# The ninth half rows of the second up projection on 64 partitions, three quarters of them loaded by GpSimd

## The chip, the cores and the metric

One NeuronCore of a Trainium2 chip runs the whole program. The metric is the device time of one execution in microseconds (us). PE is the matrix engine, DVE the vector engine, ACT the scalar engine, POOL is GpSimd, SP the engine that issues most transfers. In the profile PEld is PE's loading of weights.

## The reference

Two layers of a decoder, run twice with the same weights, for one token in each of two sequences. All data are float32.

```python
B, Sq, D = 2, 1, 576            # x
H, Sk, Dh = 32, 8192, 128       # caches: 2 x 32 x 8192 x 128, twice (K and V)
Df = 4608
def _A_ref(x, k_cache, v_cache, wq, wo):      # attention on a cache
    q = (x @ wq) as B, H, 1, Dh
    p = softmax(q . k_cache * Dh ** -0.5)
    return (p . v_cache) as B, 1, H * Dh @ wo
def _B_ref(x, w_gate, w_up, w_down):          # gated MLP
    return (gelu(x @ w_gate) * (x @ w_up)) @ w_down
x = x + _A_ref(layernorm(x), ...)
x = x + _B_ref(layernorm(x), ...)
x = x + _A_ref(layernorm(x), ...)
x = x + _B_ref(layernorm(x), ...)
```

The caches are 268 MB each and are read twice, by the first and by the third step. Gate, up and down weights are 10.6 MB each and are read twice too.

## The kernel before

The kernel streams caches and weights from HBM into one large tile, `space`, of 128 partitions by 200 KB, and computes on each piece while the next ones arrive. A planner in Python, `Arena`, decides at build time where in `space` each piece lies. Every load is an entry of a list, `queue`, in a fixed order; `pump` makes entries from the front as long as a place is free, and `done(key)` frees a piece after its last reader and pumps again. So the order of the loads on SP's queue is the order of the list, and the moment of each one is given by the reader that frees its place. `fit` looks for a place from a running position on; it is what the weights of the second MLP use.

The order is: the first attention (`plan_first`), the first MLP, the second attention (`plan_second`), the second MLP (`plan_mlp(1)`). The output projection of the second attention, `wo`, comes just ahead of the second MLP: eight transfers of 1152 KB.

The second MLP contracts over D = 576. Each of its 4608-wide weight matrices is cut in two halves of 2304 columns, which gives 1152 half rows of 9216 bytes. A partition holds nine neighbouring ones, numbered u = 0 to 8, so 128 x 9 of them. `half_rows` loads some u of all 128 partitions in one transfer. For the gate it takes u in threes (`three`), for the up projection 0 to 2, 3 to 5, and then 6, 7 and 8 alone, as the order written out in `GU` says. The transposed and normalized x stands in `xt`, 32 columns for each u, and the zeros around it let a window of 8 columns pick the side (gate or up) of the accumulator `acc` that a product is added to.

`mlp(1)` runs `norm` first (the last step is a power on GpSimd, L517, which gives `rstd`), then `all_products` (L967): for gate, then up, for each u, 2 x 4 products of a 128 x 8 window with 288 columns of weights. All of them add to the two halves of `acc`. Only after the last product, of u = 8 of the up projection, does `activate` (L976 to L989) turn each half of `acc` into a half of `hT`. Then the down products (L1004) follow, 36 groups of 128 rows in eight loads, with a few idle products (L526) between them, then the addition to x (L521) and two output transfers. The first group of down products reads the first half of `hT`.

SP issues the loads in the order of the list. Each transfer waits for the eighth one before it, because eight semaphores are used in turn, and for the readers of what lay at its place.

Of the kernel before, what the change touches and what calls it, by code (L numbers as in the profile page):

```python
# [9 lines left out]
F32 = mybir.dt.float32  # L10
# [5 lines left out]
P = 128  # L16
B = 2
# [8 lines left out]
HALF = P // 2  # L26

GH = 4
NU = 9
EQ = 512  # L30
HG = DF // 16
PAD = 6
# [90 lines left out]
def decode_layers(ctx, tc, x_in, kc, vc, wq, wo, wg, wu, wd, out):  # L123
    nc = tc.nc
    scale = DH ** -0.5

    consts = ctx.enter_context(tc.tile_pool(name="consts", bufs=1))
# [15 lines left out]


    arena = Arena()
    queue, ready, places = [], {}, {}

    def pump():
        while queue and queue[0]():
            queue.pop(0)  # L150

    def done(key):
        arena.free(key)
        pump()

    def part_at(at, n):
        return space[:, at:at + n]
# [51 lines left out]
    def weights(key, n, first, transfers):  # L209

        def make():
            at = arena.ring(key, n) if first is None else arena.fit(key, n, first)
            if at is None:
                return False
            t = ready[key] = part_at(at, n)
            transfers(t)
            return True

        queue.append(make)

    def half_rows(key, w, us, first):

        width = w.shape[1] // 2
        rows = w.rearrange("r (s w) -> (r s) w", w=width).rearrange("(p u) w -> p u w", p=P)

        def transfers(t):
            nc.sync.dma_start(t.rearrange("p (u w) -> p u w", w=width), rows[:, us[0]:us[-1] + 1, :])

        weights(key, len(us) * width, first, transfers)

    def of_half(h, k):

        width = wq.shape[1] // 2
        rows = wq.rearrange("r (s w) -> (r s) w", w=width).rearrange("(p u) w -> p u w", p=P)

        def transfers(t):
            for e in range(2):
                nc.sync.dma_start(t[e::2, :], rows[e::2, 2 * k + (h + e) % 2, :])

        weights(("wq", 1, h, k), width, None, transfers)  # L240

    def split_rows(name, w, h, u):

        rows = w[:, DF // 2 * h:DF // 2 * (h + 1)].rearrange("(m r) w -> m r w", r=NU)

        def transfers(t):
            for e in range(2):
                nc.sync.dma_start(t[e::2, :], rows[:, 5 * e + u, :])

        weights((name, 0, h, u), DF // 2, None, transfers)  # L250

    def split_middle(h):

        def transfers(t):
            for g, w in enumerate((wg, wu)):
                for e in range(2):
                    lo, n = DF // 4 * (2 * h + e), DF // 4
                    nc.sync.dma_start(
                        t[e::2, n * g:n * (g + 1)], w[:, lo:lo + n].rearrange("(m r) w -> m r w", r=NU)[:, 4, :]
                    )  # L260

        weights(("gu", 0, h), DF // 2, None, transfers)
# [136 lines left out]
    def plan_mlp(layer):  # L399
        if layer == 0:  # L400
            for h in range(2):
                for u in range(4):
                    split_rows("g", wg, h, u)
                split_middle(h)
                for u in range(4):
                    split_rows("u", wu, h, u)
        else:
            for g, (name, w) in enumerate((("g", wg), ("u", wu))):
                for us in GU[g]:
                    half_rows((name, layer, us[0]), w, us, 0)  # L410
        for rows in DOWN[layer]:
            down(layer, rows)

    plan_first()
    plan_mlp(0)
    plan_second()
    plan_mlp(1)
    pump()


    ident = consts.tile([P, P], F32, name="ident")
# [37 lines left out]

    xt = consts.tile([P, PAD + NU * 32], F32, name="xt")
    nc.vector.memset(xt, 0.0)


    acc = psum1.tile([P, 2, 512], F32, name="acc")
# [13 lines left out]
    def small(p, n):  # L480

        smalls.append(smalls.pop(0))
        return smalls[0][0:p, 0:n]
# [36 lines left out]
    def add_to_x():  # L520
        nc.vector.tensor_add(x, xps, x)  # L521
# [409 lines left out]
    def mlp(layer):  # L931
        split = layer == 0
        rstd = norm(split)
        if split:
            idle_products(3)
        hT = once.tile([P, 2, NI, 2, 2, B], F32, name="hT", tag="xc")

        def window(u, at):

            return xt[:, PAD + 32 * u - at:PAD + 32 * u - at + 4 * B]  # L940

        def split_products(h):

            steps = [(("g", layer, h, u), u, 2, (0,)) for u in range(4)] + [(("gu", layer, h), 4, 1, (0, 1))]
            steps += [(("u", layer, h, u), u, 2, (1,)) for u in range(4)]
            for key, u, sides, gs in steps:
                w = ready.pop(key).rearrange("p (k c w) -> p k c w", c=4, w=HG)
                for k in range(2):
                    g, e = (k, 0) if u == 4 else (gs[0], k)
                    for c in range(4):  # L950
                        nc.tensor.matmul(
                            acc[32 * c:32 * c + 4 * B, h, :HG], window(u, 4 * g + 2 * e), w[:, k, c, :],
                            start=(key == steps[0][0] and k == 0), stop=(key == steps[-1][0] and k == 1),
                        )
                done(key)
                if key != steps[-1][0]:
                    idle_products(1)

        def all_products():

            for g, name in enumerate("gu"):
                for us in GU[g]:
                    w = ready.pop((name, layer, us[0])).rearrange("p (u v c w) -> p u v c w", v=2, c=4, w=HG)
                    for u in us:
                        for v in range(2):
                            for c in range(4):
                                nc.tensor.matmul(  # L967
                                    acc[32 * c:32 * c + 4 * B, v, :HG], window(u, 4 * g), w[:, u - us[0], v, c, :],
                                    start=(g == 0 and u == 0), stop=(g == 1 and u == NU - 1),
                                )  # L970
                    done((name, layer, us[0]))

        def activate(v):

            o = once.tile([P, 2, HG], F32, name="o", tag="row")
            nc.scalar.activation(o[:, 0, :], acc[:, v, :HG], AF.Copy, scale=rstd)  # L976
            gu = o[:, 1, :].rearrange("p (i r) -> p i r", i=NI)
            nc.vector.transpose(gu, o[:, 0, :].rearrange("p (m i) -> p i m", i=NI))  # L978
            g = gu[:, :, 0:4]
            a = once.tile([P, NI, 4], F32, name="ga", tag="part")  # L980
            nc.vector.tensor_mul(a, g, g)
            nc.vector.tensor_scalar(a, a, 0.044715, 1.0, op0=ALU.mult, op1=ALU.add)
            nc.vector.tensor_mul(a, a, g)
            nc.scalar.activation(a, a, AF.Tanh, scale=math.sqrt(2.0 / math.pi))
            nc.vector.scalar_tensor_tensor(a, a, 1.0, g, op0=ALU.add, op1=ALU.mult)
            nc.vector.tensor_mul(a, a, gu[:, :, 4:8])
            a, to = a.rearrange("p i (e b) -> p (i e) b", b=B), hT[:, v].rearrange("p i e s b -> p (i e) s b")
            nc.vector.tensor_scalar_mul(to[:, :, 0, :], a, 0.5)
            nc.scalar.mul(to[:, :, 1, :], a, 0.5)  # L989

        if not split:
            all_products()
        for v in range(2):
            if split:
                split_products(v)
            activate(v)
        for n, rows in enumerate(DOWN[layer]):
            if n < len(IDLE[layer]):
                idle_products(IDLE[layer][n])
            w = ready.pop(("d", layer, rows[0])).rearrange("p (i c) -> p i c", c=D)  # L1000
            for k, (t, i) in enumerate(rows):
                v, e = divmod(t, 2) if split else (t % 2, t // 2)
                for c in range(4):
                    nc.tensor.matmul(  # L1004
                        xps[32 * c:32 * c + 2 * B, :], hT[:, v, i, e, :, :].rearrange("p s b -> p (s b)"),
                        w[:, k, c * CW:(c + 1) * CW],
                        start=(rows is DOWN[layer][0] and k == 0), stop=(t, i) == (NT - 1, NI - 1),
                    )
            done(("d", layer, rows[0]))
        add_to_x()  # L1010
        if layer == 0:
            idle_products(1)

    attention(0)
    mlp(0)
    attention(1)
    mlp(1)
# [29 lines left out]
```

## Time and profile before

| | us |
|---|---|
| median of 3 runs | 2686.59 (2686.56 to 2686.92) |
| profiled execution, span from first to last instruction | 2685.0 |
| what lies around the span (median less span) | 1.59 |
| DVE busy | 1806.0 (67%) |
| POOL busy | 1161.8 (43%) |
| PE busy | 914.4 (34%) |
| bytes read from HBM | 1153.18 MB, 429 GB/s over the span |

A row of the timeline gives start, duration, engine, line, operation, output and inputs, and in brackets the engine's idle time before it and what ended it. In the rows for stretches of time (windows) the columns are: stretch, its length, busy time of PE, PEld, DVE, ACT and POOL with the number of instructions, the clock granted to PE, the mean busy share of the 16 DMA engines, and GB/s. SPq and ACTq are the transfers that an engine issues. In the groups, busy time and mean duration stand between the bars, idle time before the group behind them.

### The profile page before, as it was taken

The numbers are of one execution on the slowest core, as the hardware profiler recorded it, in microseconds if no ns is written. First come the engines' busy times: TensorE is split into PE (matmuls) and PEld (weight loads), VectorE is DVE, ScalarE is ACT, GpSimd is POOL, SyncE is SP. The second block draws the span as 40 slices with busy tenths as digits, with TensorE's granted clock in tenths as the row PEclk, the third lists the DMA queues.
The fourth block names the chain that finished last, engine by engine and source line by source line (L and its number), as shares of the span: only waits on it lengthen the run. The fifth ranks groups of instructions, "written<-read, shape, count | busy, mean of one in ns | idle before, by whom it ended". The sixth has DMA issues, their size and how long they took to land. (4 is left out here: it accounts for less than half of the span.)

```text
span 2685.0 us, 17174 instructions
## 1 busy us (share of the span) xinstructions
PE 914.4 (34%) x7150; PEld 305.4 (11%) x7150; DVE 1806.0 (67%) x874; ACT 163.7 (6%) x786; POOL 1161.8 (43%) x261
## 2 busy tenths in 40 slices
PE   1323332332233233334663333233223323332356
PEld 0100010010001000111221101001000100010022
DVE  4876687677667766867037877667766776776640
ACT  0000000000000000000026000000000000000000
POOL 2543454354445444544028455445444543454420
PEclk7656666665666566566986665666566656656678
DMA  9999999999999999999999999999999999999998
GB/s 422 436 436 426 437 432 434 433 434 432 433 431 435 436 428 433 436 428 425 414 418 434 431 431 436 431 434 434 437 428 434 434 435 431 431 434 435 433 421 375
DMA packets 33950, 1154.30 MB, mean 430 GB/s; under 512 B 4152, under 2 KB 4176, under 8 KB 5968
## 3 DMA queue, kind: packets, MB, share of 16 engines
q1 hardware_dynamic: 33832, 1153.19, 99.8%
q8 instruction: 56, 0.92, 0.1%
q14 instruction: 22, 0.18, 0.0%
q10 hardware_dynamic: 40, 0.01, 0.0%
HBM read 1153.18 MB, written 0.00 MB: 429 GB/s over the span
## 5 line engine op out<-in xcount | busy, mean ns | idle before, releaser
L661 POOL TENSOR_TENSOR space<-space 128x3072 f32<-128x3072 f32 (+3 forms) x221 | 1128.6, 5107 | 1263.3 <-DVE space L644 1202.5
L644 DVE TENSOR_TENSOR space<-space,bank 128x6144 f32<-128x6144 f32 (+3 forms) x223 | 1112.7, 4991 | 560.2 <-DMA space<-in_A_k_cache_dram 496.8
L762 PE MATMUL acc<-space,prz 128*8 128x512 f32 x4096 | 594.6, 744 | 199.4 <-DMA space<-in_A_v_cache_dram 195.5
L664 DVE TENSOR_REDUCE S<-space 128x48 f32<-128x3072 f32 (+3 forms) x223 | 569.3, 2553 | 89.9 <-POOL space L661 89.6
L592 PE MATMUL bank<-qsb,pick 4*64 4x128 f32 (+1 forms) x256 | 46.3, 436 | 863.1 <-DVE space L644 853.1
L762 PEld LDWEIGHTS acc<-space,prz 128*8 128x8 f32 x4096 | 119.1, 104 | 616.3 <-issue 410.6
L784 PE MATMUL bank<-of,osb 128*32 128x2 f32 x512 | 40.9, 202 | 324.4 <-DVE osb L777 324.4
L713 ACT ACTIVATE nbs<-bank 128x2 f32<-128x2 f32 (+1 forms) x68 | 11.6, 171 | 1848.2 <-PE bank L698 1801.8
L592 PEld LDWEIGHTS bank<-qsb,pick 4*64 4x64 f32 (+1 forms) x256 | 20.7, 202 | 882.5 <-DVE space L644 863.2
L517 POOL TENSOR_TENSOR rstd<-ve,mhalf 128x1 f32<-128x1 f32 x4 | 2.2, 550 | 168.8 <-DVE ve L515 168.8
L690 PE MATMUL bank<-ident,m 128*1 128x128 f32 x68 | 19.5, 286 | 160.7 <-DVE m L688 160.5
L784 PEld LDWEIGHTS bank<-of,osb 128*32 128x32 f32 x512 | 35.9, 154 | 331.7 <-DVE osb L777 330.5
L978 DVE STREAM_TRANSPOSE o<-o 128x288 f32<-128x288 f32 x4 | 2.8, 691 | 94.5 <-ACT o L976 94.5
L729 PE MATMUL bank<-sums,unit 128*128 128x2 f32 x120 | 35.2, 363 | 87.0 <-ACT prz L721 87.0
L776 DVE TENSOR_TENSOR acc<-acc,diag 128x512 f32<-128x512 f32 x64 | 43.5, 680 | 22.0 <-PE acc L762 22.0
L721 ACT ACTIVATE prz<-S,nbs 64x128 f32<-64x128 f32 (+1 forms) x128 | 50.7, 396 | 17.3 <-POOL prz L711 14.4
L803 ACT ACTIVATE oT<-bank,rinv 32x8 f32<-32x8 f32 x110 | 28.5, 259 | 381.5 <-PE bank L784 380.8
L654 ACT ACTIVATE space<-space 128x128 f32<-128x128 f32 x164 | 48.3, 296 | 23.6 <-DVE space L644 21.7
L698 PE MATMUL bank<-m,unit 1*128 1x2 f32 (+1 forms) x136 | 39.0, 354 | 25.3 <-DVE m L696 25.3
L777 DVE TENSOR_REDUCE osb<-acc 128x128 f32<-128x512 f32 x64 | 44.3, 691 | 2.2
L521 DVE TENSOR_TENSOR x<-bank,x 128x144 f32<-128x144 f32 x4 | 1.2, 308 | 64.1 <-PE bank L1004 40.4
L729 PEld LDWEIGHTS bank<-sums,unit 128*128 128x128 f32 x120 | 30.1, 311 | 92.2 <-ACT prz L721 92.2
(73 smaller groups left out, 427.6 us busy)
## 6 DMA issues: line engine op xcount, KB each, us to landing
space<-in_A_v_cache_dram SPq DMA_DIRECT2D x8, 4096.0 KB
space<-in_A_k_cache_dram SPq DMA_DIRECT2D x6, 4096.0 KB
space<-in_A_wo_dram SPq DMA_DIRECT2D x15, 1152.0 KB
space<-in_A_k_cache_dram SPq DMA_DIRECT2D x15, 1024.0 KB
space<-in_B_w_down_dram SPq DMA_DIRECT2D x9, 1152.0 KB
space<-in_B_w_gate_dram SPq DMA_DIRECT2D x3, 3456.0 KB
space<-in_A_v_cache_dram SPq DMA_DIRECT2D x10, 1024.0 KB
space<-in_A_wq_dram SPq DMA_DIRECT2D x3, 3072.0 KB
```

The lines of the kernel that those rows point to most:

```text
L592: nc.tensor.matmul(qb[n][to, :], pick[32 * c:32 * c + 4, r:r + 1].to_broadcast([4, P // it.heads]), qsb[32 * c:32 * c + 4, (h % 4) * DH:(h ...
L644: nc.vector.tensor_tensor(out=u[:, :rows, :], in0=t[:, :rows, :], in1=qb[n].unsqueeze(1).to_broadcast([P, rows, DH]), op=ALU.mult)
L654: nc.scalar.activation(u[:, j, :], u[:, j, :], AF.Copy, accum_out=S[n][:, k * JC + j:k * JC + j + 1])
L661: nc.gpsimd.tensor_tensor(out=half, in0=half, in1=u[:, :r, DH // 2:], op=ALU.add)
L664: nc.vector.tensor_reduce(out=S[n][:, k * JC:k * JC + own_rows(n, k, m)], in_=prod.pop((n, k)), axis=AX.X, op=ALU.add)
L698: nc.tensor.matmul(mT[n][:, :heads], ones[0:1, :], m1[:, :heads], start=True, stop=True)
L721: nc.scalar.activation(pr[at, lo:].rearrange("p (g e) -> p g e", e=4)[:, 0:it.rows // 2:2, :], s[at, :it.rows].rearrange("p (g r) -> p g r ...
L729: nc.tensor.matmul(tot[n][:, :ITEMS[n].heads], ones, rs.pop(n), start=True, stop=True)
L762: nc.tensor.matmul(accumulator(n)[32 * c:32 * c + 8, :], pr[:, at:at + 8], t[g // 4][:, g % 4 * 4:g % 4 * 4 + 4, :].rearrange("p j d -> p ...
L776: nc.vector.tensor_tensor(out=q, in0=q, in1=diag.unsqueeze(2).to_broadcast([P, 4, DH]), op=ALU.mult)
L777: nc.vector.tensor_reduce(out=t, in_=q.rearrange("p r d -> p d r"), axis=AX.X, op=ALU.add)
L784: nc.tensor.matmul(po[lo:lo + 32, i, :], t[:, i::GH], of, start=True, stop=True)
```

## The change

The half row u = 8 of the second up projection is laid out anew. Its 128 rows are no longer the ninth of each partition's nine on all 128 partitions, but stand on the upper 64 partitions, two behind each other (s = 0 and 1), and are contracted in two products of 64 partitions each. Of every four partitions, SP loads the last one (two transfers of 16 rows), ahead of the other up rows; GpSimd loads the other three in 12 transfers of eight rows of 9216 bytes. Ahead of each of these GpSimd issues a transfer of 8 x 16 bytes into a small tile, `spare`. GpSimd issues all of them in `load_upper`, which stands behind `norm` in the program. The columns of `xt` for u = 8 are brought to the upper partitions by one product with `ident` and one copy on ACT. The products of these rows, `upper_products`, stand where those of u = 8 stood.

```diff
+    def upper_rows(key, w, u):
+        width = w.shape[1] // 2
+        rows = w.rearrange("r (s w) -> (r s) w", w=width).rearrange("(s a j i u) w -> s a i u j w", s=2, a=2, j=8, u=NU)
+        def transfers(t):
+            to = t[HALF:].rearrange("(a j i) (s w) -> s a i j w", a=2, j=8, s=2)
+            upper.extend((to[s, a, i], rows[s, a, i, u]) for s in range(2) for a in range(2) for i in range(3))
+            for s in range(2):
+                nc.sync.dma_start(
+                    t[HALF + 3::4, s * width:(s + 1) * width],
+                    w.rearrange("r (s w) -> (r s) w", w=width).rearrange("(s j i u) w -> s i u j w", s=2, i=4, u=NU)[s, 3, u],
+                )
+        weights(key, 2 * width, 0, transfers)
...
             for g, (name, w) in enumerate((("g", wg), ("u", wu))):
+                if name == "u":
+                    upper_rows((name, layer, NU - 1), w, NU - 1)
                 for us in GU[g]:
-                    half_rows((name, layer, us[0]), w, us, 0)
+                    if name == "g" or us[0] < NU - 1:
+                        half_rows((name, layer, us[0]), w, us, 0)
...
+        def load_upper():
+            first = small(P, 2 * B)[HALF:]
+            at = PAD + 32 * (NU - 1)
+            nc.tensor.matmul(first, ident[:HALF, :HALF], xt[:HALF, at:at + 2 * B], start=True, stop=True)
+            nc.scalar.copy(xt[HALF:, at + 32:at + 32 + 2 * B], first)
+            for n, (to, rows) in enumerate(upper):
+                nc.gpsimd.dma_start(spare[:, n % 2, :], x_in[:, 0, :].rearrange("b (j w) -> (b j) w", j=4)[:, :4])
+                nc.gpsimd.dma_start(to, rows)
+        def upper_products():
+            key = ("u", layer, NU - 1)
+            w = ready.pop(key)[HALF:].rearrange("p (s v c w) -> p s v c w", s=2, v=2, c=4)
+            for s in range(2):
+                for v in range(2):
+                    for c in range(4):
+                        nc.tensor.matmul(
+                            acc[32 * c:32 * c + 4 * B, v, :HG],
+                            xt[HALF:, PAD + 32 * (NU - s) - 4:PAD + 32 * (NU - s) + 4], w[:, s, v, c, :],
+                            start=False, stop=(s == 1),
+                        )
+            done(key)
...
         if not split:
+            load_upper()
             all_products()
```

More of the change, by code (lines that the diff above doesn't have):

```diff
@@ L145, in decode_layers @@
     arena = Arena()
-    queue, ready, places = [], {}, {}
+    queue, ready, places, upper = [], {}, {}, []
     def pump():
@@ L458, in decode_layers @@
     )
-    xt = consts.tile([P, PAD + NU * 32], F32, name="xt")
+    xt = consts.tile([P, PAD + NU * 32 + 2 * B], F32, name="xt")
     nc.vector.memset(xt, 0.0)
+    spare = consts.tile([8, 2, 4], F32, name="spare")
     acc = psum1.tile([P, 2, 512], F32, name="acc")
@@ L962, in all_products @@
                 for us in GU[g]:
+                    if name == "u" and us[0] == NU - 1:
+                        upper_products()
+                        continue
                     w = ready.pop((name, layer, us[0])).rearrange("p (u v c w) -> p u v c w", v=2, c=4, w=HG)
```

## The prediction

> **What bounds the kernel now.** I read the page first: its span, the DMA rows, and the queues.
>
> ```profile
> span 2685.0 us, 17174 instructions
> ...
> DMA  9999999999999999999999999999999999999998
> GB/s 422 436 436 426 437 432 434 433 434 432 433 431 435 436 428 433 436 428 425 414 418 434 431 431 436 431 434 434 437 428 434 434 435 431 431 434 435 433 421 375
> ...
> DMA packets 33950, 1154.30 MB, mean 430 GB/s; under 512 B 4152, under 2 KB 4176, under 8 KB 5968
> ...
> q1 hardware_dynamic: 33832, 1153.19, 99.8%
> ...
> q10 hardware_dynamic: 40, 0.01, 0.0%
> ```
>
> The DMA engines are busy in every one of the 40 slices, at 414 to 438 GB/s in all but the last. One queue, that of SP, carries 99.8% of their share; the second, ACT's, carries 40 small packets; GpSimd has no queue at all. The page gives the span, 2685.0 us; the three runs have a median of 2686.59 us, so 1.59 us lie around the span. I work on the span and carry its change over to the median.
>
> The chain of waits says the same for the end. It runs through transfers alone until the last products:
>
> ```profile
> 2581.61 22.01 DMA space<-in_A_wo_dram
> ...
> 2603.68 49.37 DMA space<-in_B_w_up_dram
> ...
> 2653.07 27.34 DMA space<-in_B_w_down_dram
> ...
> 2680.45 0.67 PE bank L1004 x16
> ...
> 2681.16 0.47 PE bank L1004 x8
> ...
> 2681.66 0.31 DVE x L521
> ```
>
> The first three rows are loads that follow each other without a gap; from the last landing it is 1.5 us to the finished x. So the time is the bytes over the rate of the 16 engines, plus whatever those engines leave unused. The bytes don't change here. What can change is the unused part, and for that I cut the last 14 us into stretches. The last two columns are the mean busy share of the 16 engines and GB/s:
>
> ```profile
> 2668.00:2670.00 2.00, 1.65 (x56) 1.52 (x60) 0.00 (x0) 0.00 (x0) 0.00 (x0) 1.00 1.01 424
> ...
> 2672.00:2673.00 1.00, 1.00 (x37) 0.86 (x30) 0.00 (x0) 0.00 (x0) 0.00 (x0) 1.00 1.04 420
> 2673.00:2674.00 1.00, 0.94 (x8) 0.18 (x3) 0.00 (x0) 0.00 (x0) 0.00 (x0) 1.00 0.95 380
> 2674.00:2675.00 1.00, 0.13 (x6) 0.12 (x10) 0.00 (x0) 0.00 (x0) 0.00 (x0) 1.00 0.80 330
> 2675.00:2676.00 1.00, 1.00 (x33) 0.81 (x26) 0.00 (x0) 0.00 (x0) 0.00 (x0) 1.00 0.66 274
> 2676.00:2677.00 1.00, 0.49 (x10) 0.05 (x8) 0.00 (x0) 0.00 (x0) 0.00 (x0) 1.00 0.59 247
> 2677.00:2678.00 1.00, 0.87 (x24) 0.49 (x24) 0.00 (x0) 0.00 (x0) 0.00 (x0) 1.00 0.46 189
> 2678.00:2679.00 1.00, 0.00 (x0) 0.00 (x0) 0.00 (x0) 0.00 (x0) 0.00 (x0) 1.00 0.55 212
> 2679.00:2680.00 1.00, 0.92 (x24) 0.54 (x24) 0.00 (x0) 0.00 (x0) 0.00 (x0) 1.00 0.43 173
> 2680.00:2681.00 1.00, 0.55 (x16) 0.33 (x16) 0.00 (x0) 0.00 (x0) 0.00 (x0) 1.00 0.07 25
> 2681.00:2682.00 1.00, 0.56 (x13) 0.11 (x8) 0.31 (x1) 0.00 (x0) 0.00 (x0) 1.00 0.00 0
> ```
>
> Until 2673 all engines work. Then the share sinks to about one half within four microseconds, stays near 0.5 from 2677 to 2680, and ends by 2680.6. That is the shape of two groups of about eight engines each: one runs out between 2673 and 2677, the other works on alone until about 2680.6. The idle part is 0.05+0.20+0.34+0.41+0.54+0.45+0.57+0.93 = 3.5 us of all 16 engines. Of these some 0.4 lie behind 2680.6; if the tail were level, the loads would end 3.1 us earlier. This is all that a shift of bytes between engines can bring, about 0.1% of the time, and it is below 0.2% of it, 5.4 us, which is about what a measurement of this kernel can tell from no change.
>
> **Part 1: what the shift does to the tail.** The ninth half row of the second up projection is one transfer of this group before:
>
> ```profile
> space<-in_B_w_up_dram SPq DMA_DIRECT2D x3, 1152.0 KB
> ```
>
> It is 128 rows of 9216 bytes, 8 on each of 16 engines. At 424 GB/s (the first row of the stretches) one engine moves 26.5 GB/s, so a row costs it 0.35 us and the transfer 2.8 us. After the change the rows stand, two behind each other, on 64 partitions: 128 rows again. SP takes the 32 of every fourth partition in two transfers of 16 rows, so 2 rows for each engine. GpSimd takes the other 96 in 12 transfers of 8 rows, each behind a dummy transfer of 8 times 16 bytes. If a transfer of 8 rows uses eight neighbouring engines, and the next one the other eight, then all dummies go to one half of the engines and all 96 rows to the other half: 12 rows on each. One half then has 14 rows where it had 8, the other has 2: +6 and -6 rows, 2.1 us each way. If the half that is relieved is the late one, it ends at 2680.6 - 2.1 = 2678.5, and the early one, whose last engine is done at about 2676.9 (the share is under 0.5 from 2677), ends at 2676.9 + 2.1 = 2679.0. The last landing comes 1.6 us earlier. The dummies bring 12 packets of 16 bytes to an engine and vanish beside 72 MB.
>
> [...]
>
> **Part 2: is the last work on the path still that transfer?** What follows the last up row on PE and the other engines:
>
> ```profile
> 2611.38 0.55 POOL L517 TENSOR_TENSOR rstd<-ve,mhalf 128x1 f32<-128x1 f32 x1 [38.01 <-DVE ve L515]
> ...
> 2614.77 4.56 PE L967 MATMUL acc<-space,xt 128*8 128x288 f32 x48 [5.19 <-DMA space<-in_B_w_gate_dram]
> ...
> 2655.88 1.16 PE L967 MATMUL acc<-space,xt 128*8 128x288 f32 x16 [1.62 <-DMA space<-in_B_w_up_dram]
> ...
> 2659.82 0.23 ACT L989 ACTIVATE hT<-ga 128x36 f32<-128x36 f32 x1 [0.49 <-DVE ga L986]
> ...
> 2662.14 4.04 PE L1004 MATMUL bank<-space,hT 128*4 128x144 f32 x72 [3.40 <-DMA space<-in_B_w_down_dram]
> ...
> 2682.00 0.64 SPq L1019 DMA_DIRECT2D out_dram<-x  x1
> ```
>
> The up products of the ninth row start at 2655.88 and the first down product at 2662.14. From there PE's groups until the end are:
>
> ```profile
> L1004 PE MATMUL bank<-space,hT 128*4 128x144 f32 x288 | 11.9, 317 | 7.1 <-DMA space<-in_B_w_down_dram 7.0
> L526 PE MATMUL bank<-prz,ident 128*4 128x256 f32 x26 | 6.4, 379 | 0.0
> ```
>
> PE waits 7.0 us for down weights in this stretch, 3.4 of it before the first product. So 3.6 us of waiting lie behind 2662.14, and the first half of hT, which the first down rows need, was ready at 2659.82 + 0.23 = 2660.05, 2.1 us ahead of them: together 5.7 us by which the end can come forward before PE is the bound. The change makes 16 products of the ninth row out of 8 (64 partitions, two half rows each); 8 products took 1.16 us, and so the path from there gets 1.2 us longer at most; 5.7 - 1.2 = 4.5 us are left, more than the 1.6 us that the transfers give. The added product and copy that bring x to the upper partitions run behind 2611, while PE waits for gate weights until 2614.77, and cost nothing; if that cover were gone they would cost about 0.6 us, by two steps like the 0.31 us of the addition to x above.
>
> **Part 3: SP's queue.** SP issues two small transfers ahead of the first up rows and drops the last one. Each of its transfers waits for the one eight before it, and for the products that used the place. The up and the down loads are issued in
>
> ```profile
> 2595.24 11.56 SPq L227 DMA_DIRECT2D space<-in_B_w_up_dram  x5
> 2617.84 38.34 SPq L271 DMA_DIRECT2D space<-in_B_w_down_dram  x8
> ```
>
> the latter so from 2617.84 to 2656.2, while the chain shows the down loads moving from 2653 on. With two transfers more in the row, and one fewer, each down load waits for an earlier transfer than before, never a later one; the places of the up rows are filled in another order, but the first is issued at 2595.24 and moves only behind the gate rows, 10.6 MB or 25 us at 424 GB/s. I book nothing here. If the queue did run dry, each microsecond would be a microsecond of the end.
>
> **Part 4: GpSimd's loads have to arrive in time.** They are issued in GpSimd's order behind rstd, which ends at 2611.93 (2611.38 + 0.55, above). Nothing of GpSimd's own is queued behind them; PE waits for them ahead of the ninth row's products, and behind those products wait the activation and all down products. The data must be there when the row's products can start, 2655.9 before. It may be later: the path from there to the finished x takes 2681.97 - 2655.88 = 26.1 us, of which 5.7 are the waits of part 2, so 20.4 us; loads that land at T end the work no earlier than T + 20.4, and this reaches the old end, 2681.97, at T = 2661.6. GpSimd has 49.7 us for 24 transfers, 2.07 us each, before it costs anything against before, and 48 us before it eats into the gain.
>
> The trace has no transfer of GpSimd. The nearest rows are the eight loads of x at the start, 1.1 KB each, which ACT issues beside SP's full queue, and their first reader:
>
> ```profile
> L140 ACTq DMA_DIRECT2D x<-in_A_x_dram x8: 238/290/543, 1.0 to 10.5; - x8
> ```
>
> ```profile
> 17.58 0.31 DVE L488 BATCH_NORM_STATS2 stats<-x 128x6 f32<-128x144 f32 x1 [12.61 <-DMA space<-in_A_wq_dram]
> ```
>
> Issue takes 0.29 us of ACT's time each. From 1.0 to 17.58, when the first reader of x starts, the eight take 16.6 us, 2.07 us each. (The row names a wq load as what ended the wait; the operation reads x alone.) Those eight ran beside rows of wq, the 24 of GpSimd run beside rows of gate and up:
>
> ```profile
> space<-in_B_w_gate_dram SPq DMA_DIRECT2D x3, 3456.0 KB
> ...
> space<-in_A_wq_dram SPq DMA_DIRECT2D x3, 3072.0 KB
> ```
>
> A row is 24.6 KB there and 27.6 KB here; if a small transfer waits for the rows in front of it, it takes 2.07 x 27.6 / 24.6 = 2.32 us. So 24 transfers take between 24 x 0.29 = 7 us, if they only need issuing, and 24 x 2.32 = 55.7 us, if they follow each other as those eight do. The latter ends at 2667.6. Transfers of both halves overlap, as each dummy waits only for the dummy two before it, and each load for the load four before it. I therefore take the middle, some 30 us, landing at about 2642; both ends stay for the range.
>
> **The sum.** Transfers -1.6 us, products 0, SP's queue 0, GpSimd 0 while it lands before 2656: span 2683.4 us, median 2686.59 - 1.6, which I give as 2685.0.
>
> **The rivals.**
> *The loads fall on the late half.* Nothing in the rows says which eight engines are late, or where the first transfer of an unused queue begins. If it goes the wrong way, the late half has 6 rows more: last landing at 2680.6 + 2.1, time 2688.7. For it: no row excludes it. Against it: the few-row transfers of x come on top for some engines, and if those are the ones that a queue starts with, the late half is the one that gets the dummies; a weak reason, as 40 packets weigh little. It decides in the tail, and from the first row.
> *GpSimd is late.* At 2.32 us for each transfer the loads land at 2667.6 and the work ends at 2688.0 where it was 2682.0: 2686.6 + 6.0 = 2692.6. It decides from 2.07 us each; at 2.30 us each the loss passes 5.4 us. For it: the x loads took as long beside a full queue. Against it: their issue alone was spread over 9.5 us (1.0 to 10.5), and GpSimd's transfers overlap.
> *No shift.* If the 8 rows are spread over all 16 engines, or the half changes with each transfer, the bytes stay level and the tail stays as it is: 2686.6, give or take 0.5. [...] For it in the trace: SP's transfers keep all 16 busy whatever their shape.
>
> **How the numbers follow.** Relief of the late half 0.46, wrong half 0.28, no shift 0.12, late GpSimd 0.14. The low end lets the relieved half give its whole 2.1 us and 0.3 more, 2684.2. The high end takes in the wrong half and the beginning of a late GpSimd, 2689.0; outside are about 0.10 for a later GpSimd and 0.05 for what I don't see. The likeliest case alone lies in 2684.2 to 2685.8. Nearly all cases are within 5.4 us of before: same 0.87. Slower by more needs GpSimd over 2.30 us each, or a cost that I don't see: 0.11. Faster by more has no mechanism here: 0.02.
>
> **What would show it.** Right: in the last stretches the share stays near 1 until about 2676 and falls within 3 us; the last down load lands near 2679; the ninth row's products wait for up rows of SP, not of GpSimd; down products start near 2661. Wrong half: the share falls earlier, and stays at one half for about 8 us. Late GpSimd: products of the ninth row start behind 2661, and PE hardly waits for down weights after them. No shift: the same tail as before. The forecast is wrong if the loads of gate and up already come later, or if the stream falls under 414 GB/s between 2612 and 2650.

## The result and the profile after

| | before | after |
|---|---|---|
| median of 4 runs each, us | 2686.57 (2686.39 to 2686.92) | 2698.55 (2697.78 to 2698.96) |
| profiled execution, span, us | 2685.0 | 2697.1 |

The ratio is 1.0044, with an interval of 1.003 to 1.0058: the change costs 12.0 us. The forecast was 2685.0, in a range that ended at 2689.0.

The page after, its span, the GB/s of the 40 slices and the two queues that matter:

```profile
span 2697.1 us, 17249 instructions
...
GB/s 420 435 434 434 433 434 434 432 434 433 432 435 432 431 432 433 434 430 425 416 416 433 431 432 435 432 432 433 435 433 435 434 434 432 432 434 430 431 409 317
...
q1 hardware_dynamic: 33752, 1152.31, 99.6%
...
q0 software_dynamic: 768, 0.89, 0.1%
```

All but the last two slices read nearly as before. The last two, which hold the second MLP, fall from 421 and 375 GB/s to 409 and 317. The new queue, q0, is that of GpSimd. Stretches of 10 us show how they fall. Two of before, with the mean busy share of the 16 DMA engines and GB/s at the end of each row:

```profile
2620.00:2630.00 10.00, 3.10 (x48) 1.22 (x48) 0.00 (x0) 0.00 (x0) 0.00 (x0) 0.90 1.00 429
2630.00:2640.00 10.00, 5.64 (x56) 1.77 (x60) 0.00 (x0) 0.00 (x0) 0.00 (x0) 0.67 0.99 424
```

and of after, with the tail behind them:

```profile
2620.00:2630.00 10.00, 4.69 (x56) 1.41 (x48) 0.00 (x0) 0.00 (x0) 2.05 (x5) 0.83 1.02 326
2630.00:2640.00 10.00, 3.43 (x32) 1.17 (x36) 0.00 (x0) 0.00 (x0) 1.85 (x4) 0.67 0.98 296
2640.00:2650.00 10.00, 2.58 (x36) 0.78 (x32) 0.00 (x0) 0.00 (x0) 1.95 (x5) 0.67 1.02 375
2650.00:2660.00 10.00, 4.55 (x48) 1.38 (x40) 0.00 (x0) 0.00 (x0) 2.75 (x6) 0.67 0.99 338
2660.00:2670.00 10.00, 8.25 (x96) 2.52 (x89) 0.00 (x0) 0.00 (x0) 1.03 (x2) 0.79 1.01 363
...
2682.00:2684.00 2.00, 2.00 (x44) 1.11 (x32) 0.00 (x0) 0.00 (x0) 0.00 (x0) 1.00 0.96 397
2684.00:2686.00 2.00, 1.86 (x44) 1.31 (x44) 0.00 (x0) 0.00 (x0) 0.00 (x0) 1.00 0.86 347
2686.00:2688.00 2.00, 1.50 (x35) 0.93 (x34) 0.00 (x0) 0.00 (x0) 0.00 (x0) 1.00 0.77 316
2688.00:2690.00 2.00, 1.40 (x30) 0.54 (x24) 0.00 (x0) 0.00 (x0) 0.00 (x0) 1.00 0.44 170
...
2690.00:2691.00 1.00, 0.00 (x0) 0.00 (x0) 0.00 (x0) 0.00 (x0) 0.00 (x0) 1.00 0.14 58
2691.00:2692.00 1.00, 0.92 (x24) 0.54 (x24) 0.00 (x0) 0.00 (x0) 0.00 (x0) 1.00 0.12 48
```

This is the main reading of the case. From 2620 to 2670 the engines are as busy as before (0.98 to 1.02) and move a fifth less: packets take longer (of those of 27,648 bytes a tenth over 1.57 us, in before over 1.03, by the packet records of the two traces). Over the six stretches from 2610 to 2670 the GB/s add up to 2116, in before to 2553; 437 x 10 us is 4.4 MB, 10.3 us at 425 GB/s, of the 12.1 us that the span grew. The tail has another shape: no long stretch at one half, but a fall from 2684 on and a last 2 us at 0.12 to 0.14, about what two engines of 16 make (0.125).

What GpSimd, PE and the end of the chain of waits do (start, duration; then one row of the waits, and the issue row with KB and median us to landing):

```profile
2612.65 0.73 POOL L986 DMA_DIRECT2D spare<-in_A_x_dram  x1
...
2619.35 0.52 POOL L986 DMA_DIRECT2D spare<-in_A_x_dram  x1 [4.43 <-DMA spare<-in_A_x_dram]
...
2661.35 0.52 POOL L987 DMA_DIRECT2D space<-in_B_w_up_dram  x1
...
2671.09 1.16 PE L996 MATMUL acc<-space,xt 64*8 64x288 f32 x16 [1.08 <-DMA space<-in_B_w_up_dram]
...
2675.32 2.39 PE L1052 MATMUL bank<-space,hT 128*4 128x144 f32 x72 [1.26 <-ACT hT L1036]
...
2680.79 2.39 PE L1052 MATMUL bank<-space,hT 128*4 128x144 f32 x72 [1.37 <-DMA space<-in_B_w_down_dram]
```

```profile
POOL spare L986 <- DMA spare<-in_A_x_dram: 36.7, 10, 5.3
```

```profile
space<-in_B_w_up_dram POOLq DMA_DIRECT2D x12, 72.0 KB, 10.5
```

```profile
2663.24 29.20 DMA space<-in_B_w_down_dram
...
2692.49 0.67 PE bank L1052 x16
...
2693.70 0.31 DVE x L541
```

GpSimd waits 10 times for a dummy, 3.7 us each, and issues its last row transfer at 2661.35; the last ninth-row products start at 2671.09. The first down products behind them wait 1.26 us for `hT`, not for weights. The end is a down load all the same, and PE waits for down weights before it.

### The profile page after: what moved, and what is told of

Its sections match the earlier page's. It is cut to its first block, busy times and chain, and to the rows that moved or that the text cites. A ratio compares the mean times of both kernels' runs of the same rounds, so it can differ in the third digit from the quotient of the medians.

```text
span 2697.1 us, 17249 instructions
## 1 busy us (share of the span) xinstructions
PE 908.1 (34%) x7168; PEld 303.9 (11%) x7168; DVE 1806.1 (67%) x874; ACT 163.8 (6%) x787; POOL 1174.3 (44%) x285
## 5 line engine op out<-in xcount | busy, mean ns | idle before, releaser
L782 PE MATMUL acc<-space,prz 128*8 128x512 f32 x4096 | 588.5, 737 | 200.2 <-DMA space<-in_A_v_cache_dram 196.2
L684 DVE TENSOR_REDUCE S<-space 128x48 f32<-128x3072 f32 (+3 forms) x223 | 569.4, 2553 | 90.3 <-POOL space L681 90.0
```

The source lines that it names most:

```text
L684: nc.vector.tensor_reduce(out=S[n][:, k * JC:k * JC + own_rows(n, k, m)], in_=prod.pop((n, k)), axis=AX.X, op=ALU.add)
L782: nc.tensor.matmul(accumulator(n)[32 * c:32 * c + 8, :], pr[:, at:at + 8], t[g // 4][:, g % 4 * 4:g % 4 * 4 + 4, :].rearrange("p j d -> p ...
```

## The experiments

Three questions were put: does the order of GpSimd's transfers choose the engines, is it GpSimd's queue, and is it the half of the partitions? Each group was measured beside its own runs of before, whose median stands with it.

### The queue and the order (before 2686.8)

**No GpSimd.** In after, SP loads all upper rows, in eight transfers of 16 rows; no dummies.

```diff
-            upper.extend((to[s, a, i], rows[s, a, i, u]) for s in range(2) for a in range(2) for i in range(3))
             for s in range(2):
-                nc.sync.dma_start(t[HALF + 3::4, ...], ...[s, 3, u])
+                for i in range(4):
+                    nc.sync.dma_start(t[HALF + i::4, ...], ...[s, i, u])
```

> The changed kernel, but all 128 rows on the upper 64 partitions are loaded by SP, in eight transfers of 16 rows; no transfer of GpSimd, no dummies. Theory Q (the software queue: GpSimd's transfers slow every engine while they are under way): the stream keeps 420 to 435 GB/s between 2612 and 2670, time 2685 to 2689. Theory P (placement: rows that land on the upper half alone, or by an engine that does not fill those partitions in a 128-row load, slow the other packets): the stream falls below 400 GB/s while these rows move, time 2692 to 2700.

Measured: 2694.1, ratio 1.0026 (1.0016 to 1.0036). Two of its stretches:

```profile
2620.00:2630.00 10.00, 5.01 (x52) 1.74 (x48) 0.00 (x0) 0.00 (x0) 0.00 (x0) 0.82 0.95 295
2630.00:2640.00 10.00, 3.09 (x28) 1.06 (x32) 0.00 (x0) 0.00 (x0) 0.00 (x0) 0.50 0.61 152
```

and the up loads as SP issues them, the small transfers first:

```profile
2595.35 42.02 SPq L240 DMA_DIRECT2D space<-in_B_w_up_dram  x8
2637.59 2.09 SPq L227 DMA_DIRECT2D space<-in_B_w_up_dram  x4
```

Two things are mixed here. In the first row the share is nearly full and the rate is down by a third: the rows slow the stream without GpSimd. In the second the share itself falls to 0.61: eight small transfers stand in a row, each transfer waits for the eighth before it, the large up loads are issued only from 2637.59, and SP's queue runs dry. After shows the first sign and not the second.

**The old layout, halves in turn.** Before, but GpSimd loads the ninth row, in 16 transfers of eight rows to the old 128 partitions, lower and upper half in turn, no dummies; once the lower half goes first, once the upper. If a transfer's place in the queue chose its engines, as the author supposed and no trace shows, the two orders would differ in which engines write which half, and one of them would lose less.

```diff
+            to = t.rearrange("(h a j i) w -> h a i j w", h=2, a=2, j=8)
+            upper.extend((to[h, a, i], rows[h, a, i, u]) for a in range(2) for i in range(4) for h in (0, 1))   # the second kernel: (1, 0)
...
+            for to, rows in upper:
+                nc.gpsimd.dma_start(to, rows)
```

> The kernel before, but GpSimd loads the ninth half row of the up projection in its old layout on 128 partitions: 16 transfers of eight rows, lower half and upper half in turn, the lower half first; no dummies. If GpSimd's transfers take eight engines in turn, this and the run with the upper half first differ only in which engines write which half. Theory Q: both lose alike, about 16/24 of the 12 us, 2693 to 2697. Theory P: one of the two keeps 420 GB/s and 2686 to 2688, the other loses, 2692 or more; I expect this one to be the good one.

> [...] Theory P: 2692 or more here if the lower half first gives 2686 to 2688, or the other way round.

Measured: 2694.36 and 2694.16, both 1.0028 (1.0017 to 1.0039 and to 1.0038). The order changes nothing, against the expectation that one of the two would be free of loss.

**The row ahead of its dummy.** After, with the two lines of the loop exchanged. If a transfer's place in the queue chose its engines, rows and dummies would each go through other ones here.

```diff
+                nc.gpsimd.dma_start(to, rows)
                 nc.gpsimd.dma_start(spare[:, n % 2, :], ...)
-                nc.gpsimd.dma_start(to, rows)
```

> [...] Theory Q: the loss stays, 2696 to 2702, with another tail. Theory P: if the rows of the changed kernel go through engines that do not fill the upper half, the loss of some 12 us shrinks to under 5 us here (2684 to 2691); if they already go through the right ones, it grows, over 2700.

Measured: 2698.7, 1.0044 (1.0029 to 1.0059), the time of after and neither of the two outcomes named for a theory of placement. With the pair above, no run shows the engines chosen by a transfer's place in the queue.

### The half of the partitions (before 2686.59)

**After on the lower half.** Everything of after mirrored: rows on partitions 0 to 63, x brought down instead of up.

```diff
-            to = t[HALF:].rearrange(...)
+            to = t[:HALF].rearrange(...)
...
-                    t[HALF + 3::4, s * width:(s + 1) * width],
+                    t[3:HALF:4, s * width:(s + 1) * width],
...
-            nc.tensor.matmul(first, ident[:HALF, :HALF], xt[:HALF, at:at + 2 * B], ...)
+            nc.tensor.matmul(second, ident[HALF:, HALF:], xt[HALF:, at:at + 2 * B], ...)
```

> The changed kernel mirrored: all its rows lie on the lower 64 partitions, the columns of x go the other way, and everything else is the same, dummies and SP's quarter too. Theory E (a transfer of eight rows always goes through the same eight engines, those that fill the lower half in a 128-row load, whatever was issued ahead of it; rows on the upper half then share the way into these partitions with the other eight engines): while GpSimd's rows move the stream keeps over 410 GB/s but for the moments of SP's two transfers, and the time is 2684 to 2689. Theory Q (GpSimd's transfers slow every engine wherever they land): the stream falls as in the changed kernel, 2696 to 2701. If the rows go through the engines of the upper half, this is the mismatched case and the loss is that of the changed kernel too.

Measured: 2690.48, 1.0014 (1.0005 to 1.0023). Its stretches:

```profile
2620.00:2630.00 10.00, 5.62 (x48) 1.65 (x48) 0.00 (x0) 0.00 (x0) 2.06 (x4) 0.66 1.02 393
2630.00:2640.00 10.00, 5.14 (x48) 1.59 (x48) 0.00 (x0) 0.00 (x0) 2.57 (x6) 0.66 0.99 380
2640.00:2650.00 10.00, 5.34 (x48) 1.64 (x48) 0.00 (x0) 0.00 (x0) 2.57 (x6) 0.66 0.99 416
```

The same transfers, dummies and queues on the other half cost 3.9 us instead of 12.0. The place alone was 8.1 us. A smaller dip is left, between 2620 and 2640, and the time lies above the 2684 to 2689 that were expected.

**Lower half, GpSimd alone.** As before it, but GpSimd loads all 16 groups of eight rows, SP none, and the dummies are gone.

```diff
-            upper.extend(... for i in range(3))
-            for s in range(2):
-                nc.sync.dma_start(...)
+            upper.extend(... for i in range(4))
...
-                nc.gpsimd.dma_start(spare[:, n % 2, :], ...)
```

> Rows on the lower 64 partitions, all 128 of them loaded by GpSimd in 16 transfers of eight, no dummies, nothing by SP. Theory E: no loss in the stream (over 415 GB/s from 2610 to 2660), eight rows more on eight engines and eight fewer on the others; 2684 to 2688. Theory Q: 16/24 of the loss, 2692 to 2697. If the engines change with each transfer, every other transfer is mismatched and the stream falls in turns, as in the runs on 128 partitions.

Measured: 2689.22, 1.001 (1.0001 to 1.0019).

```profile
2620.00:2630.00 10.00, 6.16 (x56) 1.69 (x48) 0.00 (x0) 0.00 (x0) 2.59 (x5) 0.67 1.00 427
2630.00:2640.00 10.00, 4.80 (x52) 1.47 (x48) 0.00 (x0) 0.00 (x0) 1.56 (x3) 0.82 1.00 428
...
2680.00:2682.00 2.00, 0.85 (x31) 0.49 (x24) 0.00 (x0) 0.00 (x0) 0.00 (x0) 1.00 0.12 50
2682.00:2684.00 2.00, 1.47 (x40) 0.55 (x30) 0.00 (x0) 0.00 (x0) 0.00 (x0) 1.00 0.05 20
```

While GpSimd's transfers arrive the stream is full: its queue costs nothing by itself. The 2.6 us, more than was expected, are in the tail, where a share of 0.12, about two engines, works on behind 2680.6.

**After without dummies.**

```diff
-                nc.gpsimd.dma_start(spare[:, n % 2, :], ...)
```

> The changed kernel without the dummies; rows on the upper half, SP's quarter as it was. Theory E: dummies move nothing, so the loss stays within 3 us of the changed kernel, 2695 to 2700. If dummies steer which engines are used, half of the rows go through the other engines now and the loss changes by a half, about 2692. Theory Q with a price for each transfer: half the loss, 2690 to 2694.

Measured: 2698.72, 1.0045 (1.0031 to 1.0059).

```profile
2629.22 0.52 POOL L986 DMA_DIRECT2D space<-in_B_w_up_dram  x1 [2.72 <-DMA space<-in_B_w_up_dram]
```

```profile
2620.00:2630.00 10.00, 5.22 (x48) 1.61 (x48) 0.00 (x0) 0.00 (x0) 2.07 (x4) 0.66 1.03 313
2630.00:2640.00 10.00, 1.80 (x16) 0.59 (x20) 0.00 (x0) 0.00 (x0) 0.00 (x0) 0.63 1.00 257
...
2650.00:2660.00 10.00, 5.72 (x52) 1.81 (x56) 0.00 (x0) 0.00 (x0) 0.00 (x0) 0.67 0.98 415
```

GpSimd is done issuing at 2629.7, 32 us sooner than in after, and the time is the same. So GpSimd's lateness did not set the time, and the dummies change nothing in it (2698.72 without, 2698.55 with). The loss comes in a shorter and deeper dip (257 GB/s) and is over by 2650: it belongs to the rows, not to the time over which they are spread.

**Lower half, eight rows by SP.** No GpSimd; SP loads 16 rows a transfer, two on each of eight partitions, in three groups between the gate and up loads.

```diff
-                nc.gpsimd.dma_start(to, rows)
+            for to, rows in upper[3 * n:3 * n + 3]:
+                nc.sync.dma_start(to, rows)
```

> Rows on the lower 64 partitions, all loaded by SP, in eight transfers of eight partitions with two rows each, put between the gate and up loads; GpSimd loads nothing. Theory E, and SP's transfers of eight also go through the engines of the lower half: no loss in the stream, eight rows more on those engines, eight fewer on the others. The tail is then shorter by up to 1.5 us if the others are the late ones: 2685 to 2687; or longer by 2.8 us, 2688 to 2691, if these are. If SP spreads them otherwise, rows share ways and the stream falls while they move, 2690 or more.

Measured: 2689.27, 1.001 (1.0001 to 1.0019). On the lower half SP's transfers to eight partitions cost what GpSimd's do, 2.7 against 2.6 us.

### One thing at a time (before 2686.74)

Four kernels are before with extra rows that nothing reads: six SP transfers of up half rows (of u = 0), two each behind three of the gate and up loads, to a place of their own. They differ in the half and in the rows of a transfer alone.

```diff
+            to = t[:HALF].rearrange("(a j i) w -> a i j w", a=2, j=8)
+            place.extend((to[a, i, :8], rows[0, a, i, 0, :8]) for a in range(2) for i in range(4))
```

Eight rows to the lower half, as above; to the upper half (`t[HALF:]`); four rows (`:4`) and two (`:2`) to the lower.

> The kernel before with 48 extra rows of 9216 bytes that nobody reads: six transfers of eight rows by SP, put between the gate and up loads, to the lower 64 partitions (0.44 MB more than needed). Theory E: they go through the eight engines of the lower half, six rows or 2.1 us more on each, and disturb nobody. If the late group is the other eight, the tail hides them (2686.5 to 2687.2). If two of the late engines are among these eight, as the runs with rows on the lower half suggest, two engines end 2.1 us later than the late ones did: 2688.0 to 2689.0, with a busy share of 0.12 at the end.

> The same 48 extra rows, on the upper 64 partitions. Theory E: the same eight engines now write where the other eight write, each row slows two engines and what is queued behind it, and the stream falls below 350 GB/s while they move: 2690 to 2695. If only GpSimd's transfers do harm on the wrong half, the time is that of the run with extra rows on the lower half.

> As the extra rows on the lower half, in transfers of four rows, which by theory E take the first four engines only: six rows more on each. If late engines are among these four, the time is 2688.0 to 2689.0 with a busy share of 0.06 or 0.12 in the last two us of loads; if none is, the time is that of before within 0.5 us.

> As before, in transfers of two rows, on the first two engines only. Late engines among these two: 2688.0 to 2689.0; none: before within 0.5 us. With the run of four rows it says where the late ones of the lower half sit.

| extra rows | median, us | ratio |
|---|---|---|
| 6 x 8, lower | 2688.27 | 1.0005 (0.9996 to 1.0015) |
| 6 x 8, upper | 2693.83 | 1.0027 (1.0017 to 1.0037) |
| 6 x 4, lower | 2686.55 | 0.9999 (0.999 to 1.0008) |
| 6 x 2, lower | 2686.85 | 1.0 (0.9991 to 1.001) |

Eight rows, lower half:

```profile
2620.00:2630.00 10.00, 3.10 (x48) 1.22 (x48) 0.00 (x0) 0.00 (x0) 0.00 (x0) 1.00 1.00 428
2630.00:2640.00 10.00, 4.65 (x48) 1.46 (x48) 0.00 (x0) 0.00 (x0) 0.00 (x0) 0.83 1.00 427
...
2680.00:2682.00 2.00, 0.99 (x28) 0.62 (x32) 0.00 (x0) 0.00 (x0) 0.00 (x0) 1.00 0.14 56
```

Eight rows, upper half:

```profile
2620.00:2630.00 10.00, 5.84 (x52) 1.69 (x48) 0.00 (x0) 0.00 (x0) 0.00 (x0) 0.66 1.03 362
2630.00:2640.00 10.00, 5.85 (x52) 1.65 (x48) 0.00 (x0) 0.00 (x0) 0.00 (x0) 0.67 0.99 351
2640.00:2650.00 10.00, 5.25 (x48) 1.69 (x48) 0.00 (x0) 0.00 (x0) 0.00 (x0) 0.67 0.98 362
```

Four rows, lower half:

```profile
2680.00:2682.00 2.00, 1.10 (x24) 0.44 (x24) 0.31 (x1) 0.00 (x0) 0.00 (x0) 1.00 0.06 22
```

The first two kernels differ in `HALF:` against `:HALF` alone, and by 5.6 us, with the dip of after in the second and none in the first; their intervals don't meet, while the 1.5 us of the first kernel alone is not clear of no change. The difference is 0.116 us of the whole stream for a row, 1.9 us of engine time (16 x 0.116) where the row itself takes 0.35. By after and its mirror it is less: 8.1 us for 128 rows, 0.063 a row, or 0.084 if all of it is put down to GpSimd's 96. The four-row transfers bring no straggler, the eight-row ones do (0.14 against 0.06 in 2680 to 2682): so, if four rows use four of those eight engines, which no run shows, the late ones among the eight are not these four.

## Why the prediction was wrong

**The step that failed** is in "What bounds the kernel now": "What can change is the unused part, and for that I cut the last 14 us into stretches." It took the rate of a busy engine as fixed and costed a row at 0.35 us wherever it lands. The bytes didn't change and the share stayed at 0.98 to 1.02, but the rate of busy engines fell to 296 to 375 GB/s from 2620 to 2670 (257 in one stretch without dummies). None of the rivals had this; it lay in the 0.05 "for what I don't see". Only the last sentence named it as a sign of being wrong: a stream under 414 GB/s between 2612 and 2650. It fell to 296.

**The mechanism.** Shown: most of the loss goes with the half (12.0 against 3.9 us for the mirrored kernel; 7.1 against 1.5 for the extra rows), not with the queue (SP's rows do it too), the order, or the dummies. That packets get slower is shown too: those of 27,648 bytes have a median of 1.03 us in before and 1.09 in after, and a tenth of them took over 1.03 and over 1.57, in the traces' packet records. Of the two kernels with 48 extra rows, the one on the lower half keeps 428 and 427 GB/s from 2620 to 2640 at a share of 1.00, the one on the upper half falls to 362 and 351 at 1.03 and 0.99. Theory E of the expectations is the author's explanation; 12.0 against 3.9 and 7.1 against 1.5 us are in keeping with it, but the trace does not number the engines, and no run shows which of them write which partitions. Why a row on the upper half costs 1.9 us of engine time, where the row itself takes 0.35, stays open.

**"If a transfer of 8 rows uses eight neighbouring engines, and the next one the other eight"**: no run shows the first half, though none speaks against it; the second is contradicted by the pairs in which only the order differs: row ahead of dummy 2698.7, dummy ahead 2698.55, none 2698.72; and the two orders of halves gave 2694.36 and 2694.16. The 1.6 us of the sum rest on this placement, six rows more on one half of the engines and six fewer on the other, which no run shows; what the runs showed in its place is a stream of 296 to 375 GB/s from 2620 to 2670 and a time 12.0 us longer.

**"If the half that is relieved is the late one."** The tail did change: the three microseconds near one half of before (0.43 to 0.55 from 2677 to 2680) are gone in after, and 0.12 to 0.14, about two engines, is late instead. What follows is an estimate, worked out as if all eight-row transfers used the same eight engines, which no run shows. The late engines of before, some seven by the 0.43 from 2679 to 2680, are then not one half: by the shares of the tails, two of them are among the eight that got more rows. With 8 more rows each, 8 x 0.35 = 2.8 us, the kernels on the lower half lost 2.6 and 2.7; the 6 more rows of after come to 2.1, where six unread rows more on each cost 1.5. By this estimate the relief of 1.6 us could not come, however the stream behaved.

**The sum as it came out.** 12.0 = 8.1 for GpSimd's and SP's rows on the upper half (after less its mirror) + 2.1 for the two late engines (the estimate above) + 1.8 left. With 1.5 in place of 2.1 the remainder is 2.4; the first and the last term together, 9.9 to 10.5, are near the 10.3 us that the rates gave. The remainder was not run alone. In the mirror the dip to 393 and 380 GB/s, 80 x 10 us or 1.9 us against before's 429 and 424, stands in the stretches in which SP's two transfers of 16 rows lie in after: their 32 packets run there from 2626.2 to 2636.7. In the mirror GpSimd goes on issuing to the stretch from 2650 to 2660, without another dip (416 and 433 GB/s behind 2640, in before 416 and 436). The two kernels on the lower half without such transfers have none (427 and 428 with GpSimd alone, 421 and 428 with SP's eights). So rows in transfers of 16 seem to cost on the lower half too.

**Part 2** (PE is not the bound): held at the end. The first down products wait for `hT` at 2675.32, but PE waits 1.37 us for down weights at 2680.79, and the chain ends in a down load. **Part 3** (SP's queue doesn't run dry): held, as the share stays at 0.96 to 1.00 from 2676 to 2684; the kernel with SP alone shows what the other case looks like. **Part 4** (GpSimd takes some 30 us, landing at 2642): the size was wrong. From 2612.65 to 2671.09, when the last products of these rows start, it is 58.4 us for 24 transfers, 2.4 each, above the upper bound of 2.32. That "each dummy waits only for the dummy two before it" was read as overlap, but a dummy takes 8.8 us to land in a full stream (median of its issue row), so that wait sets the pace. By the prediction's own path, landing + 20.4 us, this ends at 2691.5, 2.5 us ahead of the real end of 2694.0: late, but not what decides, as the kernel without dummies shows. The rival of a late GpSimd was thus right about the lateness and not about what decides.

**The range** failed for the same reason as the forecast: it was built from the tail and the beginning of a late GpSimd, and left the slowed stream out. With the measured 2.4 us a transfer, GpSimd's lateness alone would have ended 9.5 us behind before by the prediction's path, also outside the range.

## What to carry to other kernels

Before a transfer of few partitions is added to a full stream, try it on both halves of the partitions; here eight-row transfers were harmless to the stream on the lower 64 (421 to 428 GB/s from 2620 to 2640 in three kernels) and cost 0.06 to 0.12 us a row on the upper 64. Read the busy share beside the GB/s: in mid-stream a falling share went with a queue run dry (0.61 with SP alone), and a full share with falling GB/s with slower packets (1.02 at 326 GB/s in after). And measure which engines are late, with a few unread rows, before bytes are shifted to level a tail: no version here beat the kernel before, and a shift of rows onto the engines of the four-row transfers, where 24 unread rows cost nothing (2686.55), was not tried; it would bring an estimated 2 x 0.35 = 0.7 us, if these are always the same four and each of the other twelve gives up two rows.

## What was not expected of the hardware

- Rows on the upper half slow packets of other loads (in after a tenth of those of 27,648 bytes over 1.57 us, in before over 1.03): 48 rows, 0.44 MB, cost 5.6 us more there than on the lower half.
- Six unread transfers of eight rows to the lower half left a share of 0.14, about two engines, at work from 2680 to 2682, the same six of four rows 0.06, before 0.03; why these engines are late was not settled.
- A GpSimd transfer costs 0.52 us of its issue time, against 0.29 on ACT's rows of x, and a dummy of 128 bytes takes 8.8 us to land beside a full queue.
